# Sign features, v halves and gate taps at the start of an attention, mixing and gating kernel

## The chip, the cores and the metric

The kernel runs on one core of a Trainium2 chip. The core has TensorE (PE, matrix products), VectorE (DVE), ScalarE (ACT), GpSimd (POOL) and SyncE (SP), which here issues the DMA transfers. The metric is the device time of one execution in microseconds. Of the kernel before there are three timed runs: 687.34, 683.41 and 684.14 us, with a median of 684.14.

## The reference

Three layers follow each other, in float32, for a batch of 2.

1. Attention with 8 heads, 768 positions and head size 64. Each q and k row gets a bucket from the signs of its products with six projection vectors, and a score counts only where the buckets of q and k are equal:

```
q_bits = (einsum('bhsd,dk->bhsk', q, proj) > 0);  k_bits likewise
mask   = bucket(q_bits)[:, :, :, None] == bucket(k_bits)[:, :, None, :]
scores = where(mask, q @ k.T / 8, -1e9);  attn = softmax(scores);  x = attn @ v
```

2. A mixing layer on x (768 by 512 for each batch entry): the real part of a Fourier transform over both axes is added to x, then layer norm, a product with w_ch1, relu, a product with w_ch2, and an addition.

3. A gate: a causal convolution over 5 positions with taps conv_w, a sigmoid, times x @ w_val, and a product with w_out.

## The kernel before

Products are exact enough because each float32 operand is split into an upper and a lower fp16 half: the upper half is a rounded copy (`copy_of`, lines 110 to 117), the lower half the rest (`rest_of`, lines 122 to 126). On VectorE the lower half is one instruction; on GpSimd (`"g"`) it is two, a scaling of the input in place and a subtraction. `split` (line 128) does both halves; its string says on which engine each is done ("a" ScalarE, "v" VectorE, "g" GpSimd).

Attention goes over pairs of heads (`g`, four of them in a batch entry), over three units `i` of 256 query rows, over the two heads `hh`, and over two tiles `j` of 128 rows. For each tile, `pair` (line 317) makes scores on TensorE, a row maximum on VectorE (line 338), an exponential on ScalarE (line 343), an upper half on ScalarE and a lower half on GpSimd, and has them transposed, mostly by a DMA that SP issues (line 355). `unit_out` (line 358) multiplies by v and writes x.

Before the first tile of a pair its operands are prepared. `ta` holds the lower parts of q and k and, in 32 rows each, the sign features: they enter the score product, so that unequal buckets get a large penalty. For pairs 1 to 3 this is `prep` (line 230); for pair 0 of batch 0 `prep_first` (line 280) does it head by head. In `prep_first`, for each head: the halves of q and k, their transposes on TensorE, products with the projection (line 307), the sign features by comparison (line 314, one VectorE instruction for head 0, two for head 1), and a copy of 32 rows (line 315) that completes the operand of that head. This copy is kept as a mark, `marks["first", 0]` and `marks["first", 1]`; the exponentials of tiles 0 and 1 are marks too (`marks["first", 2]` and `3`, line 343, on ScalarE). `values` (line 270) makes the halves of v.

The order of the instructions on each engine is worked out ahead of time by a planner, which takes what is ready, earlier lines of the program first. `after_mark` (line 158) names an instruction behind which the ones of its block are to be queued. In the kernel before, the halves of v of pair 0 stand under `marks["first", 0]` (line 273), and so does the splitting in `prep` of pair 1 (line 232); head 1's sign features stand under none, since `MF` is 0 (line 311). The loads of the constants cf, cs and the taps stand under the mark of pair 1's last transposed copy (line 947). `REST` (`'vv'` for batch 0) says on which engine the lower halves of q and k are made, `VH` (`'gg'` for batch 0) the halves of v of pairs 1 to 3. `widen` (line 417) turns the taps from the 64-bit form of the input into float32 with three VectorE instructions; it stands ahead of the loop over the attention of batch 0 (line 962).

The loads of q, k and v of a pair take three buffers, so the load of the next pair's q waits until the last reader of a buffer is done.

Of the kernel before, what the change touches and what calls it, by code (L numbers as in the profile page):

```python
# [15 lines left out]
QS = 2.0 ** 5  # L16
PS = 2.0 ** 3
VS = 2.0 ** 6
# [46 lines left out]
VH = ('gg', 'av')  # L65
PF = 0
MF = 0
PJE = 'g'
REST = ('vv', 'gv')
# [8 lines left out]
def attention_fft_mix_gated_kernel(  # L78
# [31 lines left out]
    def copy_of(o, i, s, eng):  # L110
        if eng == "a":
            return nc.scalar.activation(out=o, in_=i, func=ACTF.Copy, scale=s)  # L112
        if eng == "g":
            return nc.gpsimd.tensor_scalar(o, i, s, 1.0, ALU.mult, ALU.mult)
        if isinstance(s, float) and s == 1.0:
            return nc.vector.tensor_copy(out=o, in_=i)
        return nc.vector.tensor_scalar(o, i, s, None, ALU.mult)  # L117

    def both(o, i0, i1, op, eng):
        return (nc.gpsimd if eng == "g" else nc.vector).tensor_tensor(out=o, in0=i0, in1=i1, op=op)  # L120

    def rest_of(l, h, i, s, eng="v"):
        if eng == "g":
            copy_of(i, i, s, "g")
            return both(l, i, h, ALU.subtract, "g")
        return nc.vector.scalar_tensor_tensor(out=l, in0=i, scalar=s, in1=h, op0=ALU.mult, op1=ALU.subtract)  # L126

    def split(h, l, i, s, how):

        unit = isinstance(s, float) and s == 1.0  # L130
        if len(how) == 3:
            if not unit:
                copy_of(i, i, s, how[0])
            s, unit, how = 1.0, True, how[1:]
        copy_of(h, i, s, how[0])
        if unit:
            return both(l, i, h, ALU.subtract, how[1])
        return rest_of(l, h, i, s, how[1])
# [10 lines left out]
    cw = const.tile([128, KC, K], INT32, name="cw")  # L149
# [5 lines left out]
    moved, last, marks = {}, [], {}  # L155

    @contextmanager
    def after_mark(ins):
        with ExitStack() as stack:
            for i in ins:  # L160
                stack.enter_context(tc.issue_after(i))
            yield


    class Pool:
# [8 lines left out]
        def widen(self, stack, bufs):  # L174
            self.more, self.extra = stack.enter_context(tc.tile_pool(name="q_" + self.name, bufs=bufs, reuse_waits="tile", **self.kw)), bufs
            stack.callback(self.narrow)
# [23 lines left out]
    def attention(b, P, after=None):  # L200
# [15 lines left out]
        def move(o, i, eng):  # L216
            if eng in "vga":
                copy_of(o, i, 1.0, eng)
            else:
                nc.sync.dma_start(out=o, in_=i)  # L220
# [9 lines left out]
        def prep(g):  # L230
            lq, lk, lv = ld.pop(g)
            with after_mark([marks["first", PF]] if not b and g == 1 else []):
                st = [P.a.tile([128, 2 * C, 2, D], FP16, tag="a", name="st", lasting=b and g == 0) for _ in range(2)]
                for y, x in enumerate((lq, lk)):
                    copy_of(st[y][:, :, 1 - y, :], x, QS, "a")
                for y, x in enumerate((lq, lk)):
                    rest_of(st[y][:, :, y, :], st[y][:, :, 1 - y, :], x, QS, REST[b][y])
            if b and g == 2:
                tb = P.spare.tile([128, 2, 2, S], FP16, tag="tb", name="tb")
            else:  # L240
                tb = P.tb.tile([128, 2, 2, S], FP16, tag="tb", name="tb", lasting=b and g == 0)
            ta = P.ta.tile([128, 2, 2, S], FP16, tag="ta", name="ta", lasting=b and g == 0)
            for y in range(2):
                it = st[y].rearrange("p c x d -> p (c x d)")
                if (b, g) in PPE:
                    marks[b, "prep", g] = by_pe(tb[:, y].rearrange("p h t -> p (h t)"), it, PPE[b, g])
                else:
                    marks[b, "prep", g] = nc.sync.dma_start_transpose(
                        out=tb[:, y].rearrange("p h (c t) -> p (h c) t", t=128), in_=it
                    ).ins  # L250
            move(ta[0:64, 0], tb[64:128, 0], QJ[b][0])
            move(ta[0:64, 1], tb[0:64, 1], QJ[b][1])
            for n in range(2):
                r = slice(n * 384, n * 384 + 384)
                bt = P.bt.tile([128, 512], FP32, tag="g", name="bt")[:, 0:384]
                for x in range(3):
                    for hh in range(2):
                        for y in range(2):
                            o = 64 * hh + 32 * y
                            nc.tensor.matmul(  # L260
                                out=bt[o:o + 32, :], lhsT=pj[:, x, y, :], rhs=tb[:, y, hh, r], start=(x == 0), stop=(x == 2)
                            )
                for hh in range(2):
                    o = slice(64 * hh, 64 * hh + 64)
                    nc.vector.tensor_scalar(ta[64:128, 0, hh, r], bt[o, :], lim[o, 0:1], lim[o, 1:2], ALU.is_gt, ALU.mult)
            move(ta[64:96, 1], ta[96:128, 0], QJ[b][2])
            values(g, lv)
            tq[g] = ta, tb

        def values(g, lv):  # L270
            vt = P.vt.tile([128, 2, C, 2, D], FP16, tag="vt", name="vt")
            v2 = vt.rearrange("p h c x d -> p (h c) x d")
            with after_mark([marks["first", PF]] if not b and g == 0 else []):
                split(v2[:, :, 0, :], v2[:, :, 1, :], lv, VS, 'av' if not b and g < 1 else VH[b])
            va[g] = vt

        def first_tiles():
# [2 lines left out]
        def prep_first(hh):  # L280

            ta, tb = tq[0]
            lq, lk, _ = ld[0]
            for y, x in enumerate((lq, lk)):
                if y == 0:
                    p = P.tp.tile([128, 1024], FP16, tag="tp", name="stp")
                else:
                    p = (P.pv if hh else P.bt).tile([128, 1024], FP16, tag="pv" if hh else "g", name="stp")
                x = x[:, hh * C:hh * C + C]
                st = P.a.tile([128, 2 * C, 2, D], FP16, tag="a", name="st")[:, 0:C]  # L290
                copy_of(st[:, :, 1 - y, :], x, QS, "a")
                rest_of(st[:, :, y, :], st[:, :, 1 - y, :], x, QS)
                for c in range(C):
                    nc.tensor.transpose(p[:, c * 128:c * 128 + 128], st[:, c].rearrange("p x d -> p (x d)"), P.idh)
                copy_of(tb[:, y, hh], p[:, 0:S], 1.0, EVF[y][hh])
                copy_of(ta[0:64, y, hh], tb[64 - 64 * y:128 - 64 * y, y, hh], 1.0, SH[2 * hh + y])
            o = slice(64 * hh, 64 * hh + 64)
            if hh:
                bt = [P.tp.tile([128, 512], FP32, tag="tp", name="bt")[:, 0:384] for _ in range(2)]
            else:  # L300
                b2 = P.sc.tile([128, 2, 512], FP32, tag="sc", name="bt")[:, :, 0:384]
                bt = [b2[:, n] for n in range(2)]
            for n in range(2):
                for x in range(3):
                    for y in range(2):
                        i = o.start + 32 * y
                        nc.tensor.matmul(
                            out=bt[n][i:i + 32, :], lhsT=pj[:, x, y, :], rhs=tb[:, y, hh, n * 384:n * 384 + 384],
                            start=(x == 0), stop=(x == 2),
                        )  # L310
            with after_mark([marks["first", MF]] if hh and MF else []):
                t2 = ta[64:128, 0, hh, :].rearrange("p (n r) -> p n r", n=2)
                for w, i in [(t2[:, n], bt[n][o]) for n in range(2)] if hh else [(t2, b2[o])]:
                    nc.vector.tensor_scalar(w, i, lim[o, 0:1], lim[o, 1:2], ALU.is_gt, ALU.mult)
            marks["first", hh] = copy_of(ta[64:96, 1, hh], ta[96:128, 0, hh], 1.0, "v").ins
# [574 lines left out]
    if True:  # L890
# [10 lines left out]
        cwd = tmp.tile([128, KC, K, 2], INT32, name="cwd")  # L901
        cwt = tmp.tile([128, KC, K], INT32, name="cwt")
# [44 lines left out]
        with tc.issue_after(marks[EARLY]):  # L947
# [11 lines left out]
                pre=[work.tile([128, 4 * WP], INT32, tag="t4", name="pre", bufs=4) for _ in range(NPRE)],  # L959
            )  # L960
            next(w)
        widen(cw, cwd[:, :, :, 0], cwd[:, :, :, 1], cwt)
        for i, _ in enumerate(a0):
            if (i % STEP == W0 % STEP and i >= W0) if PACE else i % 4:
                next(w, None)
            if i in (A1LD, A1AT):
                next(a1)
# [136 lines left out]
```

## Time and profile before

| | us |
|---|---|
| median of three timed runs | 684.14 |
| the profiled execution, in all | 682.82 |
| its span, first to last instruction | 681.0 |
| TensorE busy in the span | 578.8 |
| VectorE busy | 521.9 |
| ScalarE busy | 367.0 |
| GpSimd busy | 283.4 |

The profile is of one execution. Busy times are sums over all stages; a table by windows of time shows which engine is full in which stage. A row of a timeline has the start, the duration, the engine, the line of the kernel, the operation, what is written and read, and in brackets how long the engine was idle before and what ended this.

### The profile page before, as it was taken

How to read it: one execution, taken by the hardware profiler on the slowest of the kernel's cores; microseconds unless marked ns; L12 is line 12 of the kernel's file. 1: busy time of each engine (PE TensorE's matmuls, PEld its weight loads, DVE VectorE, ACT ScalarE, POOL GpSimd, SP SyncE). 2: the span in 40 equal slices, each digit the busy share in tenths (PEclk: the TensorE clock that was granted, in tenths of full speed). 3: DMA queues.
4: the chain of work that ended last, by engine and by line, in shares of the span. 5: the costliest groups of instructions: out<-in, count | busy, mean ns of one | idle time of the engine just before them, and what ended most of it. 6: DMA issues, size and time to landing. Idle time of an engine off the chain costs nothing.

```text
span 681.0 us, 13258 instructions
## 1 busy us (share of the span) xinstructions
PE 578.8 (85%) x5078; PEld 443.7 (65%) x5078; DVE 521.9 (77%) x1007; ACT 367.0 (54%) x752; POOL 283.4 (42%) x312
## 2 busy tenths in 40 slices
PE   6787767866537789986999999988999999999997
PEld 3454535544324657665677788877677788888864
DVE  6978797799999898998865369996999256282682
ACT  4997979996764337875888426311334202111242
POOL 3868668875864415767656301260232100000000
PEclk8787779787866689999999999998799999999999
DMA  8989999989776354689785764000000000000001
GB/s 300 236 139 234 210 234 217 225 133 179 149 153 139 110 124 109 148 155 198 139 145 102 135 183 151 6 1 1 1 32 32 32 1 2 2 1 1 1 32 63
DMA packets 177888, 75.84 MB, mean 111 GB/s; under 512 B 162464, under 2 KB 168224, under 8 KB 177824
## 3 DMA queue, kind: packets, MB, share of 16 engines
q1 hardware_dynamic: 177248, 74.88, 50.6%
q8 instruction: 40, 0.66, 0.4%
q14 instruction: 24, 0.20, 0.1%
q10 hardware_dynamic: 576, 0.10, 0.1%
HBM read 32.50 MB, written 3.15 MB: 52 GB/s over the span
## 4 chain that ended last, share of the span: by engine, by line
PE 30%; DVE 13%; ACT 3%; issue 3%; POOL 1%; ACTq 0%; DVEq 0%; POOLq 0%
PE f L729 14%; PE f L712 8%; DVE gt L754 3%; PE op L873 2%; PE vp L848 1%; PE vp L770 1%; ACT a L112 1%; PE op L795 1%; DVE x L126 1%; DVE gt L117 1%; DVE h L694 1%; ACT e L343 1%; DVE cen L644 1%; PE mp L601 1%; DVE gt L821 1%
## 5 line engine op out<-in xcount | busy, mean ns | idle before, releaser
L120 POOL TENSOR_TENSOR a<-e,a 128x384 f16<-128x384 f32 x184 | 174.9, 976 | 93.0 <-ACT a L112 75.7
L712 PE MATMUL f<-un,w 128*128 128x256 f16 x1152 | 135.3, 274 | 3.2 <-DVE h L694 2.7
L729 PE MATMUL f<-h,w 128*128 128x256 f16 x1152 | 133.1, 274 | 0.9 <-DVE h L694 0.9
L712 PEld LDWEIGHTS <-w 128*128 128x128 f16 x1152 | 112.7, 98 | 22.0 <-issue 4.8
L729 PEld LDWEIGHTS <-w 128*128 128x128 f16 x1152 | 112.2, 98 | 17.8 <-issue 3.2
L338 DVE TENSOR_SCALAR_CACHE_REDUCE e<-sc 128x768 f32<-128x768 f32 x96 | 90.5, 949 | 16.1 <-POOL a L120 12.6
L364 PE MATMUL pv<-at,vt 128*64 128x256 f16 x864 | 75.3, 323 | 26.4 <-DMA at<-a 23.4
L343 ACT ACTIVATE e<-e,mx 128x768 f32<-128x768 f32 x96 | 89.1, 929 | 3.7
L364 PEld LDWEIGHTS <-vt 128*64 128x64 f16 x864 | 58.0, 130 | 44.7 <-issue 23.7
L112 ACT ACTIVATE a<-e 128x768 f16<-128x768 f32 x96 | 80.1, 839 | 1.0
L326 PE MATMUL sc<-ta 96*128 96x384 f16 x192 | 51.4, 352 | 29.8 <-DVE e L338 26.0
L694 DVE SCALAR_TENSOR_TENSOR h<-f,h 128x512 f16<-128x512 f32 x48 | 32.7, 686 | 32.7 <-ACT h L693 32.6
L326 PE MATMUL sc<-tb 128*128 128x384 f16 x192 | 51.9, 353 | 0.0
L693 ACT ACTIVATE h<-f 128x512 f16<-128x512 f32 x48 | 28.4, 591 | 43.1 <-PE f L712 42.9
L326 PEld LDWEIGHTS <-ta 96*128 96x128 f16 x192 | 17.0, 100 | 51.1 <-issue 44.6
L700 DVE SCALAR_TENSOR_TENSOR xb<-f,xb 128x256 f32<-128x256 f32 x24 | 13.7, 615 | 43.6 <-PE f L729 43.6
L120 POOL TENSOR_TENSOR w<-wt,w 128x256 f16<-128x256 f32 x40 | 30.1, 764 | 35.4 <-ACT w L112 35.2
L112 ACT ACTIVATE x<-xb 128x256 f16<-128x256 f32 x24 | 11.7, 535 | 54.0 <-DVE xb L700 53.5
L420 DVE SCALAR_TENSOR_TENSOR wt<-ring,wt 128x256 int32<-128x256 int32 (+1 forms) x60 | 37.0, 623 | 0.6
L821 DVE SCALAR_TENSOR_TENSOR gt<-xb,cw,gt 128x256 f32<-128x256 f32 x60 | 37.2, 680 | 0.0
L112 ACT ACTIVATE wt<-wt 128x256 f32<-128x256 f32 x40 | 16.2, 412 | 37.7 <-DVE wt L421 36.7
L421 DVE SCALAR_TENSOR_TENSOR wt<-ring,wt 128x256 int32<-128x256 int32 (+1 forms) x60 | 35.7, 602 | 0.5
(147 smaller groups left out, 930.6 us busy)
## 6 DMA issues: line engine op xcount, KB each, us to landing
ring<-in_moe_w_ch_dram SPq DMA_DIRECT2D x40, 256.0 KB, 3.1
ring<-in_moe_w_ch_dram SPq DMA_DIRECT2D x12, 512.0 KB, 5.0
lv<-in_v_dram SPq DMA_DIRECT2D x8, 384.0 KB, 4.5
out_dram<-ob SPq DMA_DIRECT2D x12, 256.0 KB, 2.0
lq<-in_q_dram SPq DMA_DIRECT2D x7, 384.0 KB, 3.9
lk<-in_k_dram SPq DMA_DIRECT2D x7, 384.0 KB, 4.6
ring<-in_moe_w_val_dram SPq DMA_DIRECT2D x4, 512.0 KB, 5.6
ring<-in_moe_w_out_dram SPq DMA_DIRECT2D x4, 512.0 KB, 3.9
```

The lines of the kernel that those rows point to most:

```text
L112: return nc.scalar.activation(out=o, in_=i, func=ACTF.Copy, scale=s)
L120: return (nc.gpsimd if eng == "g" else nc.vector).tensor_tensor(out=o, in0=i0, in1=i1, op=op)
L326: nc.tensor.matmul(out=s[:, n, 0:384], lhsT=z[0:rows, 0, hh, r], rhs=z[0:rows, 1, hh, n * 384:n * 384 + 384], start=(x == 0), stop=(x == 1),)
L338: nc.vector.tensor_scalar(e.rearrange("p (a b) -> p a b", a=2), s, -(PEN * PEN) / 2, None, ALU.max, ALU.max, accum_out=m[:, 0:1]).ins
L343: marks["first", 2 + j] = nc.scalar.activation(out=e, in_=e, func=ACTF.Exp, bias=m[:, 1:2], scale=SC, accum_out=sums[:, hh, j:j + 1]).ins
L364: nc.tensor.matmul(out=p[64 * hh:64 * hh + 64, :], lhsT=va[g][:, hh, c, x, :], rhs=at[hh][:, :, y, c, :], start=(c == 0 and n == 0), stop= ...
L420: nc.vector.scalar_tensor_tensor(out=tmp, in0=hi, scalar=-0x40000000, in1=tmp, op0=ALU.bitwise_and, op1=ALU.bitwise_or)
L421: return nc.vector.scalar_tensor_tensor(out=dst, in0=lo, scalar=29, in1=tmp, op0=ALU.logical_shift_right, op1=ALU.bitwise_or)
L694: nc.vector.scalar_tensor_tensor(out=h[:, 1, f:f + 2, :], in0=p, scalar=0.0, in1=h[:, 0, f:f + 2, :], op0=ALU.max, op1=ALU.subtract)
L712: nc.tensor.matmul(out=p[:, o, :], lhsT=w1[:, i, kd, (f + o) * 128:(f + o) * 128 + 128], rhs=un[:, j, kd, :], start=(k == 0), stop=(k == 3 ...
L729: nc.tensor.matmul(out=p[:, o, :], lhsT=w2[:, i, f, (d + o) * 128:(d + o) * 128 + 128], rhs=h[:, j, f, :], start=(k == 0), stop=(k == 3 * ...
L821: nc.vector.scalar_tensor_tensor(out=o, in0=src, scalar=cw[:, d, j:j + 1].bitcast(FP32), in1=o, op0=ALU.mult, op1=ALU.add)
```

## The change

Head 1's sign features in `prep_first` now stand under `marks["first", 0]`. v's halves of pair 0 are written out: the upper half on ScalarE under `marks["first", 0]`, the lower half on VectorE under `marks["first", 2]`. v's halves of pair 1 are made on GpSimd and VectorE instead of GpSimd alone. The lower half of pair 1's q is made on GpSimd, that of k stays on VectorE. The widening of the taps is put eight steps into the loop over batch 0's attention.

```
@@ prep
-                    rest_of(st[y][:, :, y, :], st[y][:, :, 1 - y, :], x, QS, REST[b][y])
+                    rest_of(st[y][:, :, y, :], st[y][:, :, 1 - y, :], x, QS, 'gv'[y] if not b and g == 1 else REST[b][y])
@@ values
-            with after_mark([marks["first", PF]] if not b and g == 0 else []):
-                split(v2[:, :, 0, :], v2[:, :, 1, :], lv, VS, 'av' if not b and g < 1 else VH[b])
+            if not b and g == 0:
+                with after_mark([marks["first", 0]]):
+                    copy_of(v2[:, :, 0, :], lv, VS, "a")
+                with after_mark([marks["first", 2]]):
+                    rest_of(v2[:, :, 1, :], v2[:, :, 0, :], lv, VS)
+            else:
+                split(v2[:, :, 0, :], v2[:, :, 1, :], lv, VS, 'gv' if not b and g == 1 else VH[b])
@@ prep_first
-            with after_mark([marks["first", MF]] if hh and MF else []):
+            with after_mark([marks["first", 0]] if hh else []):
@@ the loop over batch 0's attention
-        widen(cw, cwd[:, :, :, 0], cwd[:, :, :, 1], cwt)
         for i, _ in enumerate(a0):
+            if i == 8:
+                widen(cw, cwd[:, :, :, 0], cwd[:, :, :, 1], cwt)
```

## Rows read from the trace of the kernel before

**Rows 1.** The page's first part: busy us, share of the span, instructions.
```profile
PE 578.8 (85%) x5078; PEld 443.7 (65%) x5078; DVE 521.9 (77%) x1007; ACT 367.0 (54%) x752; POOL 283.4 (42%) x312
```

**Rows 2.** Windows, start:end and length; PE, PEld, DVE, ACT, POOL busy; clock, DMA, GB/s.
```profile
14.40:31.80 17.40, 13.31 (x82) 6.53 (x80) 16.11 (x33) 16.90 (x35) 12.54 (x13) 0.70 0.98 264
31.80:57.00 25.20, 20.07 (x180) 14.44 (x182) 18.51 (x37) 24.43 (x54) 17.98 (x21) 0.77 0.93 175
...
520.00:600.00 80.00, 79.63 (x707) 68.93 (x705) 40.86 (x78) 16.09 (x30) 3.33 (x3) 1.00 0.02 8
```

**Rows 3.** VectorE's timeline, 9.8 to 16.5 us.
```profile
9.80 0.74 DVE L116 COPY ta<-tb 64x768 f16<-64x768 f16 x2 [0.45 <-ACT tb L112]
...
10.84 1.07 DVE L314 TENSOR_SCALAR ta<-bt,lim 64x768 f16<-64x768 f32 x1 [0.29 <-PE bt L307]
...
11.94 1.29 DVE L314 TENSOR_SCALAR ta<-bt,lim 64x384 f16<-64x384 f32 x2
...
13.26 0.35 DVE L116 COPY ta<-ta 32x768 f16<-32x768 f16 x1
13.64 0.96 DVE L126 SCALAR_TENSOR_TENSOR vt<-lv,vt 128x768 f16<-128x768 f32 x1
14.52 0.17 DVE L419 TENSOR_SCALAR cwt<-cwd 128x20 int32<-128x20 int32 x1
...
15.53 0.96 DVE L338 TENSOR_SCALAR_CACHE_REDUCE e<-sc 128x768 f32<-128x768 f32 x1
...
16.41 0.95 DVE L126 SCALAR_TENSOR_TENSOR st<-lq,st 128x768 f16<-128x768 f32 x1
```

**Rows 4.** TensorE's timeline: the first scores, and the transposes of pair 1's q.
```profile
13.66 0.48 PE L326 MATMUL sc<-ta 96*128 96x384 f16 x2 [2.12 <-DVE ta L116]
13.99 0.49 PE L326 MATMUL sc<-tb 128*128 128x384 f16 x2
...
17.78 1.49 PE L226 MATMUL atp<-idh,st 128*128 128x128 f16 x12
```

**Rows 5.** ScalarE's timeline: v, pair 1's q and k, a marked copy, an upper half.
```profile
8.23 0.84 ACT L112 ACTIVATE vt<-lv 128x768 f16<-128x768 f32 x1 [0.73 <-DMA lv<-in_v_dram]
8.98 0.79 ACT L112 ACTIVATE tb<-stp 128x768 f16<-128x768 f16 x1
14.41 0.84 ACT L112 ACTIVATE st<-lq 128x768 f16<-128x768 f32 x1 [4.63 <-DMA lq<-in_q_dram]
15.45 0.84 ACT L112 ACTIVATE st<-lk 128x768 f16<-128x768 f32 x1 [0.20 <-DMA lk<-in_k_dram]
...
23.50 0.81 ACT L112 ACTIVATE tb<-atp 128x768 f16<-128x768 f16 x1
...
27.43 0.85 ACT L112 ACTIVATE a<-e 128x768 f16<-128x768 f32 x1
```

**Rows 6.** SP's timeline: the issues of cf and of the next v.
```profile
3.51 0.47 SPq L948 DMA_DIRECT2D cf<-in_dft_f_dram  x1
...
14.66 0.38 SPq L213 DMA_DIRECT2D lv<-in_v_dram  x1
```

**Rows 7.** GpSimd's timeline: first lower half, pair 1's v, and q in batch 1.
```profile
18.75 2.01 POOL L120 TENSOR_TENSOR a<-e,a 128x384 f16<-128x384 f32 x2 [9.83 <-ACT mx L342]
...
23.75 0.83 POOL L114 TENSOR_SCALAR lv<-lv 128x768 f32<-128x768 f32 x1
24.66 1.65 POOL L120 TENSOR_TENSOR vt<-lv,vt 128x768 f16<-128x768 f32 x1
...
125.74 2.23 POOL L120 TENSOR_TENSOR st<-lq,st 128x768 f16<-128x768 f32 x1
```

**Rows 8.** VectorE's timeline: k's lower half in batch 1, beside GpSimd's q.
```profile
124.98 1.49 DVE L126 SCALAR_TENSOR_TENSOR st<-lk,st 128x768 f16<-128x768 f32 x1 [0.77 <-ACT st L112]
```

**Rows 9.** Two idle times further on, VectorE's and ScalarE's.
```profile
40.06 0.62 DVE L380 TENSOR_TENSOR xb<-pv,xb 128x256 f32<-128x256 f32 x1 [3.92 <-ACT xb L112]
...
59.16 0.60 ACT L112 ACTIVATE w<-wt 128x512 f16<-128x512 f32 x1 [2.12 <-DVE wt L421]
```

## The prediction

> **What bounds the kernel now.** I read the page's busy line first: TensorE 85%, VectorE 77%, ScalarE 54%, GpSimd 42% over 681.0 us [rows 1]. An average over unlike stages says little, so I went on to the table by windows [rows 2]. The reader is to see that the full engine changes: from 14.4 to 57 us it is ScalarE, 16.90 of 17.40 us and then 24.43 of 25.20; near the end, from 520 to 600, it is TensorE, 79.63 of 80. The change touches none of the late work. All it edits lies in the first 30 us, so what it can do is move the beginning of attention in batch 0, and what is gained there has to pass through ScalarE's full queue.
>
> The timelines of the engines at the start show the path. VectorE does the sign features of head 0 (10.84, 1.07 us), then both halves of head 1's (11.94 to 13.23), and only then the 32-row copy that completes head 0's operand (13.26) [rows 3]. The first score matmul waits for this copy until 13.66, an idle of 2.12 us on TensorE [rows 4]. Behind the copy VectorE does v's lower half (13.64, 0.96 us), the first piece of the taps (0.17), head 1's copy and the other taps, and only at 15.53 the first row maximum, though its four score matmuls ended at 14.48 (13.99 + 0.49) [rows 3, 4].
>
> **Sign features of head 1.** The mark is a VectorE instruction and so are the two held instructions, so it takes hold. They leave the way of head 0's copy: 13.23 - 11.94 = 1.3 us.
>
> **v's lower half.** The diff puts it under a mark that is a ScalarE instruction (the exponential of the first tile), while the lower half runs on VectorE. Does such a mark hold? The kernel before has the same pattern twice. The loads of cf, cs and the taps stand under the mark of the second pair's last transposed copy, which ScalarE ran at 23.50; SP issued cf at 3.51 [rows 5, 6]. And v's upper half on ScalarE stood under the VectorE mark of 13.26 and ran at 8.23 [rows 3, 5]. So a mark orders its own engine alone. The edit therefore doesn't move v's lower half back; it takes away the hold that it had, and it can go as soon as v's upper half is done (8.23 + 0.84 = 9.07). It costs 0.96 us wherever it lands. In VectorE's hole at 9.36 to 9.80, ahead of the copies at 9.80, it pushes these by 0.5 us, of which 0.29 is absorbed by the idle before 10.84: head 0's copy is 0.2 later. Behind 10.84 it costs the copy the whole 0.96. Bounds of both edits together: 1.3 - 0.96 = 0.3 to 1.3 - 0.2 = 1.1 us. I take 1.1, the first place, since ScalarE runs v's upper half before the copy (8.98) that the VectorE copies at 9.80 wait for, so the lower half is ready before they are [rows 3, 5]. Its end also frees the buffer for the next v: SP issued that load at 14.66, right behind it [rows 6]; it now goes earlier, behind the loads of q and k in the same queue.
>
> **First maximum.** With head 0's copy at 12.2 to 12.5 and four score matmuls of 0.82 us together, the scores end at 13.4. VectorE still has 1.3 us of head 1's signs: the maximum starts near 13.9, not 15.53, 1.6 us earlier.
>
> **Taps.** Three instructions of about 0.17 us leave the stretch from 14.52 [rows 3]: some 0.5 us. Nothing reads them before the gating, after the whole of attention and mixing; where they go they cost at most those 0.5.
>
> **Swap of q and v in pair 1.** v's upper half stays on POOL. POOL loses the scaling and the subtraction of the lower half (0.83 + 1.65 us at 23.75 and 24.66) and takes the same two for q: nothing in sum, but q's come while POOL is idle, since its first lower half starts at 18.75 after 9.83 us of idle [rows 7]. q's upper half ends at 15.25 [rows 5], so they run 15.25 to 17.7. VectorE loses 0.95 us at 16.41 and takes 0.96 later, plus what the two engines cost each other: a lower half of this shape takes 0.95 alone (16.41) and k's 1.49 beside the same POOL pair in batch 1 (124.98), and POOL's subtraction 2.23 instead of 1.65 [rows 3, 7, 8]. That is +0.54 on VectorE and +0.58 on POOL. VectorE in sum: -0.95 + 0.96 + 0.54 - 0.5 = 0.05; bounds -1.5 (no mutual cost, v's in the hole at 36) to +1.4 (k's lower half held from 16.29 to the end of POOL's subtraction, 17.7).
> The Trainium skill, page "SBUF — State Buffer", section "Who interferes with whom", says that a VectorE instruction with two SBUF inputs and a GpSimd one that reads SBUF exclude each other: the later one blocks for the whole of the first. The rows of batch 1 agree: 124.98 starts inside POOL's copy, and POOL's subtraction is longer by about as much as what was left of it. By that rule k's lower half would pay 1.4 here and not 0.54.
>
> q's lower half is ready at 17.7 instead of 17.36. TensorE's transposes of it stood at 17.78 [rows 4], so this is hidden; if POOL took 0.58 more, they wait 0.5 us. The load of the next q goes the same 0.4 us later.
>
> **What of it reaches the end.** ScalarE takes the first maximum, but it has to make the upper halves of pair 1's q and k as well, which wait for DMA until 14.41 and 15.45 [rows 5]. From 14.40 to 31.80 it is idle for 0.50 us, from 31.80 to 57 for 0.77 [rows 2]. An earlier maximum fills these 0.50 (0.20 of it stands before 15.45, most of the rest before the first maximum's use); it can't make ScalarE's own work shorter. The other 0.77 belongs to later waits. Nor does POOL's relief reach further: v's pieces (to 24.66 + 1.65 = 26.3) hold up the third tile's lower half, but the first unit needs the fourth tile as well, whose upper half ScalarE ends at 27.43 + 0.85 = 28.3 whatever POOL does [rows 5, 7]. So of 1.6 us I keep **0.5**, with bounds 0 and 1.3 (0.50 + 0.77), if the queues stay as they are. On the profiled execution, 681.0 span and 682.82 in all, this is 682.3. That execution lies 1.3 below the median of 684.14, which the result is compared with: 684.14 - 0.5 = **683.6**, own range 682 to 685.5. It is no change that a measurement could tell: that needs about 0.5%, 3.4 us.
>
> **Rivals.**
> *A hole further on closes (faster).* The queues are ordered ahead of time, and moving three VectorE instructions and four POOL ones reorders what follows. VectorE stands 3.92 us at 40.06 for the first unit's output while its next maxima could run, and ScalarE 2.12 at 59.16 for weights that VectorE had not yet widened [rows 9]. If the first unit's output no longer blocks the maxima, that is 3.9 + 0.5: 684.14 - 4.4 = 679.7; with the second hole 677.6. For it: v's two POOL pieces stand just ahead of the third tile's lower half. Against: the fourth tile, above, and a hole that closes can open again elsewhere. Chance 0.30.
> *The marks hold after all.* v's lower half then waits for the first exponential (16 to 17), the next v's load goes from 14.66 to some 17.3, and pair 1's v that much later; the maximum still gains. 683.9. Chance 0.07.
> *The two engines exclude each other.* k's lower half and pair 1's v each pay 1.4: 684.14 + 2.9 - 0.5 = 686.5. For it, the rows of batch 1; against, k's high half may be planned behind. Chance 0.06. This is what the page named above would make of it.
> *TensorE waits for POOL's q (slower).* In TensorE's queue q's twelve transposes (17.78) stand ahead of later scores [rows 4]. If POOL's queue has the first tile's lower half (18.75, 2.01 us) [rows 7] before q's two pieces, these end at 20.76 + 2.48 = 23.2 and the scores stand still for 23.2 - 17.78 = 5.4 us: 684.14 + 5.4 - 0.5 = 689.0. It decides from the point where q's subtraction ends after 18.7. Against: q lands at 14.41, 3 us before the first high half. Chance 0.12.
>
> **How the numbers follow.** The forecast holds 0.45, the rivals 0.30, 0.07, 0.06 and 0.12. Faster is the first rival, 0.30. Slower is the last, 0.12, and 0.03 for the upper part of the exclusion. The rest, 0.55, is no change. The range goes down to 677.6 (both holes) and up to 688.0, short of the last rival's 689.0.
>
> **What would show it.** Head 0's last copy at 12.2 to 12.9, the first score matmul right behind it, the first maximum by 14.2. v's lower half before 13 us, not after the first exponential. q's POOL pieces before the first tile's lower half, and k's lower half longer than 0.95. ScalarE full from 14.4 to 31.8 with less than 0.3 us idle. The prediction is wrong if ScalarE's exponentials at 30 to 60 us are more than 1.3 us earlier, if the wait of VectorE for the first unit's output is gone, or if TensorE waits for the transposes of q.

## The result and the profile after

The changed kernel takes 689.85 us (median of 7 runs, 688.65 to 691.79), the kernel before 683.41 (7 runs, 682.68 to 687.34) beside it. The ratio is 1.0081, with a 95% interval of 1.0061 to 1.0102: slower by 0.8%, about 5.5 us (the ratio, here and below, is not quite that of the medians, which differ by 6.4 us here). The forecast was 683.6 us and no change; its range ended at 688.0. The profiled execution has a span of 689.9 us, before 681.0.

The page's busy line answers to [rows 1]: the work is the same (the counts are equal), but VectorE is busy for 6.6 us more and GpSimd for 2.6, TensorE for 3.1 less.

```profile
PE 575.7 (83%) x5078; PEld 439.8 (64%) x5078; DVE 528.5 (77%) x1007; ACT 367.6 (53%) x752; POOL 286.0 (41%) x312
```

VectorE's timeline of the first 27 us, and the first unit's output, answers to [rows 3, 9].

```profile
9.12 0.94 DVE L126 SCALAR_TENSOR_TENSOR vt<-lv,vt 128x768 f16<-128x768 f32 x1
...
12.22 0.18 DVE L424 TENSOR_SCALAR cwt<-cwd 128x20 int32<-128x20 int32 x1 [0.29 <-DMA cwd<-in_conv_t_dram]
12.43 0.35 DVE L116 COPY ta<-ta 32x768 f16<-32x768 f16 x1
12.82 1.29 DVE L319 TENSOR_SCALAR ta<-bt,lim 64x384 f16<-64x384 f32 x2
14.14 0.18 DVE L425 SCALAR_TENSOR_TENSOR cwt<-cwd,cwt 128x20 int32<-128x20 int32 x1
14.35 0.35 DVE L116 COPY ta<-ta 32x768 f16<-32x768 f16 x1
14.74 0.18 DVE L426 SCALAR_TENSOR_TENSOR cw<-cwd,cwt 128x20 int32<-128x20 int32 x1
14.95 0.96 DVE L343 TENSOR_SCALAR_CACHE_REDUCE e<-sc 128x768 f32<-128x768 f32 x1
...
16.71 2.38 DVE L126 SCALAR_TENSOR_TENSOR st<-lk,st 128x768 f16<-128x768 f32 x1
...
25.44 1.24 DVE L126 SCALAR_TENSOR_TENSOR vt<-lv,vt 128x768 f16<-128x768 f32 x1
...
41.30 0.62 DVE L385 TENSOR_TENSOR xb<-pv,xb 128x256 f32<-128x256 f32 x1 [4.36 <-ACT xb L112]
```

GpSimd's timeline answers to [rows 7]. q's two pieces come ahead of the first tile's lower half, as forecast.

```profile
15.72 0.84 POOL L114 TENSOR_SCALAR lq<-lq 128x768 f32<-128x768 f32 x1 [6.90 <-ACT st L112]
16.64 1.65 POOL L120 TENSOR_TENSOR st<-lq,st 128x768 f16<-128x768 f32 x1
18.79 1.96 POOL L120 TENSOR_TENSOR a<-e,a 128x384 f16<-128x384 f32 x2 [0.50 <-ACT a L112]
```

TensorE's timeline answers to [rows 4]. The fourth tile's scores now stand ahead of q's transposes (in the kernel before, behind them), and neither waits for GpSimd.

```profile
17.19 0.85 PE L331 MATMUL sc<-ta 96*128 96x384 f16 x2
...
18.47 1.19 PE L226 MATMUL atp<-idh,st 128*128 128x128 f16 x12
```

ScalarE's timeline answers to [rows 5]: the upper halves of pair 1's q and k still wait for their loads, and the first exponential stands behind them.

```profile
14.80 0.84 ACT L112 ACTIVATE st<-lq 128x768 f16<-128x768 f32 x1 [5.86 <-DMA lq<-in_q_dram]
15.84 0.84 ACT L112 ACTIVATE st<-lk 128x768 f16<-128x768 f32 x1 [0.20 <-DMA lk<-in_k_dram]
...
16.81 0.93 ACT L348 ACTIVATE e<-e,mx 128x768 f32<-128x768 f32 x1
```

It starts no earlier than in the kernel before:

```profile
16.76 0.94 ACT L343 ACTIVATE e<-e,mx 128x768 f32<-128x768 f32 x1
```

The windows of the attention's start answer to [rows 2] (start:end and length; PE, PEld, DVE, ACT, POOL busy; clock, DMA, GB/s). ScalarE has 1.01 us idle in the first, where it had 0.50, and 2.65 in the second, where it had 0.77.

```profile
14.40:31.80 17.40, 11.10 (x77) 5.75 (x76) 15.63 (x27) 16.39 (x34) 13.36 (x14) 0.83 0.94 247
31.80:57.00 25.20, 16.85 (x152) 10.87 (x149) 20.16 (x40) 22.55 (x50) 16.01 (x19) 0.77 0.86 170
```

So the front part came out much as forecast: v's lower half at 9.12, head 0's copy at 12.43, q on GpSimd early. Only 1.24 us of the loss (41.30 against 40.06) stand at the first unit's output. The rest has to be looked for later. Three views of one line each show the stages: the additions of batch 0's mixing (first and last start), those of batch 1's, and the start of batch 1's first products with w_ch2, its mixing layer's second weight matrix (in a window from 536 to 554 us). Before:

```profile
L609 DVE TENSOR_TENSOR xb<-mp,xb x12: 591/606/625, 212.1 to 239.8; 128x256 f32<-128x256 f32 x12
...
L609 DVE TENSOR_TENSOR xb<-mp,xb x12: 590/610/631, 447.0 to 471.1; 128x256 f32<-128x256 f32 x12
...
L729 PE MATMUL f<-h,w x132: 272/273/273, 539.6 to 553.9; 128*128 128x256 f16 x132
```

After:

```profile
L614 DVE TENSOR_TENSOR xb<-mp,xb x12: 597/614/639, 220.7 to 239.9; 128x256 f32<-128x256 f32 x12
...
L614 DVE TENSOR_TENSOR xb<-mp,xb x12: 591/615/630, 452.3 to 478.1; 128x256 f32<-128x256 f32 x12
...
L734 PE MATMUL f<-h,w x55: 272/273/273, 548.1 to 554.0; 128*128 128x256 f16 x55
```

Batch 0's mixing ends at the same time. Batch 1's ends 7.0 us later, and its products with w_ch2 start 8.5 later; the span is 8.9 longer. So at these products nearly all of the loss is there, and most of it shows hundreds of microseconds behind the edits.

### The profile page after: what moved, and what is told of

The parts are those of the page before. It is cut to its first block, busy times and chain, and to the rows that moved or that the text cites. A ratio compares the mean times of both kernels' runs of the same rounds, so it can differ in the third digit from the quotient of the medians.

```text
span 689.9 us, 13261 instructions
## 1 busy us (share of the span) xinstructions
PE 575.7 (83%) x5078; PEld 439.8 (64%) x5078; DVE 528.5 (77%) x1007; ACT 367.6 (53%) x752; POOL 286.0 (41%) x312
## 4 chain that ended last, share of the span: by engine, by line
PE 38%; DVE 25%; issue 3%; DMA 3%; ACT 2%; POOL 1%; SPq 0%; ACTq 0%; DVEq 0%; POOLq 0%
PE f L734 14%; PE f L717 12%; DVE wt L425 2%; DVE gt L759 2%; PE op L878 2%; PE pv L369 2%; DVE e L343 2%; DVE z L120 2%; PE sc L331 2%; DVE wt L426 2%; DVE cen L649 1%; PE vp L853 1%; DVE wt L424 1%; PE vp L775 1%; DVE h L699 1%
## 5 line engine op out<-in xcount | busy, mean ns | idle before, releaser
L717 PE MATMUL f<-un,w 128*128 128x256 f16 x1152 | 137.5, 276 | 2.6 <-DVE h L699 2.0
L369 PE MATMUL pv<-at,vt 128*64 128x256 f16 x864 | 70.3, 310 | 29.2 <-DMA at<-a 26.1
L369 PEld LDWEIGHTS <-vt 128*64 128x64 f16 x864 | 55.6, 125 | 47.2 <-issue 24.4
L120 POOL TENSOR_TENSOR w<-wt,w 128x256 f16<-128x256 f32 x40 | 31.9, 803 | 40.2 <-ACT w L112 40.2
L331 PEld LDWEIGHTS <-ta 96*128 96x128 f16 x192 | 17.9, 101 | 43.5 <-issue 36.7
L425 DVE SCALAR_TENSOR_TENSOR wt<-ring,wt 128x256 int32<-128x256 int32 (+1 forms) x60 | 40.3, 678 | 0.5
L426 DVE SCALAR_TENSOR_TENSOR wt<-ring,wt 128x256 int32<-128x256 int32 (+1 forms) x60 | 37.0, 622 | 0.5
```

The costliest lines, as they stand in the source:

```text
L331: nc.tensor.matmul(out=s[:, n, 0:384], lhsT=z[0:rows, 0, hh, r], rhs=z[0:rows, 1, hh, n * 384:n * 384 + 384], start=(x == 0), stop=(x == 1),)
L369: nc.tensor.matmul(out=p[64 * hh:64 * hh + 64, :], lhsT=va[g][:, hh, c, x, :], rhs=at[hh][:, :, y, c, :], start=(c == 0 and n == 0), stop= ...
L425: nc.vector.scalar_tensor_tensor(out=tmp, in0=hi, scalar=-0x40000000, in1=tmp, op0=ALU.bitwise_and, op1=ALU.bitwise_or)
L426: return nc.vector.scalar_tensor_tensor(out=dst, in0=lo, scalar=29, in1=tmp, op0=ALU.logical_shift_right, op1=ALU.bitwise_or)
L717: nc.tensor.matmul(out=p[:, o, :], lhsT=w1[:, i, kd, (f + o) * 128:(f + o) * 128 + 128], rhs=un[:, j, kd, :], start=(k == 0), stop=(k == 3 ...
```

## The experiments

The theories at the start. A: the time is lost because the planner, given other instructions at the start, orders everything behind them anew. B: GpSimd's q holds VectorE's k. C: the hold on v that the edit takes away was worth something. D: a moved step does harm where it now stands.

First, a reading of the two programs: with v's two new marks left out (and its old one), every engine gets the changed kernel's order, instruction by instruction. The marks on another engine do nothing, as the prediction held.

**One edit alone, ordered by the planner.** Four kernels, each before with one edit:

```
s_sign    with after_mark([marks["first", 0]] if hh else []):         # head 1's sign features
s_vfree   v's halves of pair 0 under no mark
s_q       rest_of(..., 'gv'[y] if not b and g == 1 else REST[b][y])   # q's lower half, pair 1
s_v1      split(..., 'gv' if not b and g == 1 else VH[b])             # v's lower half, pair 1
```

> The kernel before with the hold on head 1's sign features alone. Theory A (the loss comes with the new order of the queues, not with the work of an edit): an irregular change between -5 and +7 us, though the first maximum comes 1 us earlier. Theory B (the loss is GpSimd's q, which blocks VectorE's k): no loss, -1 to +0.5 us, since q and v of pair 1 are untouched. Theory C (the loss is the lost hold of v's lower half): no loss either, -1 to +0.5 us.

> The kernel before with the hold on v's halves of pair 0 taken away, nothing else. Theory A: irregular, between -5 and +7 us. Theory B: -1 to +0.5 us. Theory C: most of the loss, +4 to +7 us.

> The kernel before with pair 1's q lower half on GpSimd, nothing else. Theory A: irregular, between -5 and +7 us. Theory B: most of the loss, +4 to +7 us, with k's lower half at about 2.4 us instead of 0.95. Theory C: -1 to +1 us.

> The kernel before with the lower half of pair 1's v on VectorE, nothing else. Theory A: irregular, between -5 and +7 us. Theories B and C: a gain of up to 1 us or nothing, since 2.5 us leave GpSimd's full stretch.

| | median us | ratio to before, 95% |
|---|---|---|
| s_sign | 689.46 | 1.0086 [1.0051, 1.0121] |
| s_vfree | 695.33 | 1.0164 [1.0129, 1.0198] |
| s_q | 688.64 | 1.0077 [1.0054, 1.0099] |
| s_v1 | 699.99 | 1.0233 [1.0195, 1.0271] |

Each of these edits alone costs about as much as the whole change, or more. Their sum is 5.6%, the whole, which moves the taps as well, costs 0.8%; prices of steps would add. s_vfree (11 us) and s_v1 (16 us) even lie above the range that was expected by theory A, which ended at +7. s_sign and s_vfree run exactly before's instructions, so there an order alone is paid for. That speaks for A, but a local harm (C, D) is not excluded yet.

**The same edits in the order of before.** A helper fixes each engine's order by chaining its instructions; only the instructions under test are moved in the list.

```
for x, y in zip(q, q[1:]):        # q: one engine's instructions in the wanted order
    tc.add_manual_dep(y, x.name, NoSync)
...
VectorE in before  signs h0, signs h1, copy h0, v, tap, copy h1, tap, tap, max 1, q, max 2, k, max 3
o_sign             signs h0, copy h0, signs h1, v, tap, copy h1, tap, tap, max 1, q, max 2, k, max 3
o_early            v (at 9 us), signs h0, copy h0, signs h1, copy h1, max 1, q, max 2, k, taps, max 3
o_all              as o_early; q on GpSimd; v of pair 1 on VectorE behind the sixth maximum
o_qv               as before; q on GpSimd; v of pair 1 as in o_all
```

> Every engine's queue held in the order that the kernel before has, but for one step: head 0's operand copy goes ahead of head 1's two sign features, as in the single edit that cost 0.86%. Theory A (the loss is the new order further down the queues): no loss, -1.5 to +0.7 us against the kernel before. Theory D (the moved step itself does the harm, by what it sets off on the chip): the same loss as the single edit, +4 to +7 us.

> As o_sign, and v's lower half of pair 0 goes where the changed kernel has it (ahead of the copies at 9.8 us), and the taps go behind pair 1's k. Theory A: -2 to +0.5 us. Theory D: +4 to +12 us, as the single edits cost 0.86% and 1.64%.

> All of the changed kernel's work, with the steps of o_early, q's lower half of pair 1 on GpSimd ahead of its first tile, v's lower half of pair 1 on VectorE behind the sixth maximum, and all other queues in the order of the kernel before. Theory A: -2 to +1.5 us (the upper end is k's lower half held for 1.4 us by GpSimd). Theory D: +4 to +8 us, like the change.

> The swap of q and v of pair 1 alone, in the order of the kernel before. Theory A: -1 to +1.5 us. Theory B (the loss is GpSimd's q beside VectorE's k): +4 to +7 us. Theory D: +4 to +17 us, as the single edits of q and v cost 0.77% and 2.33%.

o_sign: 683.92 us, 0.9998 [0.9977, 1.0019]. o_early: 683.75, 0.9993 [0.9976, 1.0010]. o_all: 688.15, 1.0056 [1.0036, 1.0077]. o_qv: 687.59, 1.0042 [1.0022, 1.0062].

Beside s_sign and s_vfree this settles C, and D for three steps: the sign step, the freed v and the taps cost nothing where they stand, and gain nothing that shows. The local gain is there, and it shrinks at once: in o_early the first maximum is at 14.00 against 15.53 [rows 3], the first unit's output at 39.71 against 40.06 [rows 9], and batch 0's last mixing addition starts at 239.9 against 239.8. VectorE of o_early:

```profile
14.00 0.96 DVE L337 TENSOR_SCALAR_CACHE_REDUCE e<-sc 128x768 f32<-128x768 f32 x1
...
39.71 0.61 DVE L379 TENSOR_TENSOR xb<-pv,xb 128x256 f32<-128x256 f32 x1 [3.92 <-ACT xb L112]
```

The swap, however, costs 0.4 to 0.6% even in the old order: 2.9 us (o_qv) and 3.8 (o_all), above the ranges of theory A, which ended at +1.5, and a little below those of B and D. VectorE's timeline of o_all shows the places (k's lower half, the taps, the third maximum, pair 1's v):

```profile
16.31 2.38 DVE L126 SCALAR_TENSOR_TENSOR st<-lk,st 128x768 f16<-128x768 f32 x1 [0.45 <-ACT st L112]
18.61 0.88 DVE L418 TENSOR_SCALAR cwt<-cwd 128x20 int32<-128x20 int32 x1
19.53 0.84 DVE L419 SCALAR_TENSOR_TENSOR cwt<-cwd,cwt 128x20 int32<-128x20 int32 x1
20.40 0.80 DVE L420 SCALAR_TENSOR_TENSOR cw<-cwd,cwt 128x20 int32<-128x20 int32 x1
21.12 0.94 DVE L337 TENSOR_SCALAR_CACHE_REDUCE e<-sc 128x768 f32<-128x768 f32 x1
...
26.66 1.42 DVE L126 SCALAR_TENSOR_TENSOR vt<-lv,vt 128x768 f16<-128x768 f32 x1
```

In o_qv, where k comes later, the instructions that stand beside q's pieces pay instead, a copy of 0.35 us and a tap of 0.18:

```profile
15.05 0.87 DVE L116 COPY ta<-ta 32x768 f16<-32x768 f16 x1
15.96 1.52 DVE L419 SCALAR_TENSOR_TENSOR cwt<-cwd,cwt 128x20 int32<-128x20 int32 x1
...
19.48 0.95 DVE L126 SCALAR_TENSOR_TENSOR st<-lk,st 128x768 f16<-128x768 f32 x1
```

**The swap in parts, and the order alone.** o_allt is o_all with the taps before head 1's copy, beside an idle GpSimd; o_qt is the same without v of pair 1; o_v1 is o_early with v of pair 1 alone. l_qv is o_early's work in the planner's own order.

```
o_allt, o_qt   ..., signs h1, taps, copy h1, max 1, max 2, k, max 3, ...
l_qv           sign features held, v's mark removed, taps at step 8 of the loop; no order given
```

> As o_all (all of the change's work, each queue in the order of before), but the three taps instructions stand before head 1's 32-row copy, where GpSimd is idle, and not behind pair 1's k. Theory 1, the swap's price is paid at the places where VectorE meets GpSimd: in o_all the taps took 0.88, 0.84 and 0.80 us beside GpSimd's first lower halves instead of 0.17 each, so they return to 0.17 and the third maximum to about 19.1 instead of 21.1; k's lower half still takes 2.4. 688.15 - 2.0 = 686.2 us. Theory 2, the price lies in what the swap does to the other queues (GpSimd's later work, TensorE's wait for q): the time stays at 688.

> Order of before, with the sign features behind head 0's copy, v's lower half freed, the taps before head 1's copy, and of the swap only q's lower half of pair 1 on GpSimd; pair 1's v stays on GpSimd whole. Theory 1: k's lower half takes 2.4 instead of 0.95, q's 0.96 leaves VectorE, the taps stand 0.5 ahead of the first maximum: 683.75 + 1.45 - 0.96 + 0.5 = 684.7 us. Theory 2, q on GpSimd holds up TensorE's transposes and with them the scores: 686.5 or more.

> As o_early (sign features, v's lower half and taps moved, order of before) with only pair 1's v changed: its lower half on VectorE behind the sixth maximum, its upper half on GpSimd. Theory 1: the lower half meets GpSimd's first-tile work there, as in o_all where it took 1.42, and delays the next maxima by that: 683.75 + 1.4 = 685.2 us. Theory 2, GpSimd's relief of 0.83 + 1.65 us lets the next lower halves come sooner: 682.5 to 683.7.

> The same work as o_early (sign features held, v's lower half freed, taps eight steps into the loop, no swap), in the planner's own new order. Theory A, the order behind the first 30 us costs: 688 to 695 us, against 683.75 for o_early with the same instructions. Rival: the single edits alone were unlucky draws that cancel when they come together: 683 to 685.

o_allt: 686.72 us, 1.0034 [1.0016, 1.0052]. o_qt: 686.33, 1.0019 [1.0004, 1.0035]. o_v1: 685.78, 1.0023 [1.0006, 1.0041]. l_qv: 689.46, 1.0076 [1.0052, 1.0099].

Over o_early (0.9993) q's half costs 0.26% or 1.8 us and v's half 0.30% or 2.1 us; both together 0.41% or 2.8 us, and the taps in a bad place bring that to 0.63% in o_all, though the intervals of o_all and o_allt overlap. These differences are hardly larger than their noise, and in q's half there is also the place of the taps, which in o_qt put the first maximum at 14.66 and in o_early stand behind k. The traces support them: the first unit's output stands at 39.71 in o_early, at 41.12 in o_qt and at 41.83 in o_v1. VectorE of o_qt:

```profile
41.12 0.62 DVE L379 TENSOR_TENSOR xb<-pv,xb 128x256 f32<-128x256 f32 x1 [3.93 <-ACT xb L112]
```

v's half is a little above theory 1's 1.4 us: it meets GpSimd's lower halves of the exponentials, takes 1.63 us instead of 0.95, and one of them in turn seems held (2.50 us for two, 1.78 for the two before). VectorE in o_v1:

```profile
25.58 1.63 DVE L126 SCALAR_TENSOR_TENSOR vt<-lv,vt 128x768 f16<-128x768 f32 x1
```

GpSimd in o_v1:

```profile
25.48 2.50 POOL L120 TENSOR_TENSOR a<-e,a 128x384 f16<-128x384 f32 x2 [1.44 <-ACT a L112]
```

And l_qv beside o_early is theory A with equal instructions: 0.8% for an order.

**Where q's half is paid in the old order.** In o_qt k's lower half takes 2.21 us, but TensorE stands as well: q's transposes wait for GpSimd, and the fourth tile's scores are queued behind them. TensorE of o_qt:

```profile
17.99 1.46 PE L226 MATMUL atp<-idh,st 128*128 128x128 f16 x12 [0.87 <-POOL st L120]
19.25 0.84 PE L325 MATMUL sc<-ta 96*128 96x384 f16 x2
```

VectorE of o_qt:

```profile
16.54 2.21 DVE L126 SCALAR_TENSOR_TENSOR st<-lk,st 128x768 f16<-128x768 f32 x1
...
20.77 0.96 DVE L337 TENSOR_SCALAR_CACHE_REDUCE e<-sc 128x768 f32<-128x768 f32 x1 [1.14 <-PE sc L325]
```

In o_qlate k stands behind the third maximum, where GpSimd has ended its subtraction.

```
o_qt           max 1, max 2, k, max 3, max 4
o_qlate        max 1, max 2, max 3, k, max 4
```

> As o_qt (order of before; q's lower half of pair 1 on GpSimd), but k's lower half stands one place later in VectorE's queue, behind the third maximum, so that it meets only the end of GpSimd's subtraction. It should take about 1.2 us instead of 2.2, and the third maximum should start at 16.9 to 17.1 instead of 18.67. Theory V, VectorE's block is the price: 686.3 - 1.3 = 685.0 us. Theory P, TensorE's queue is the price (the fourth tile's scores stand behind the transposes of q, which wait for GpSimd until 17.9): the fourth maximum stays at 20.8 and the time at 686.3.

VectorE of o_qlate:

```profile
17.09 0.96 DVE L337 TENSOR_SCALAR_CACHE_REDUCE e<-sc 128x768 f32<-128x768 f32 x1 [0.65 <-PE sc L325]
18.09 0.96 DVE L126 SCALAR_TENSOR_TENSOR st<-lk,st 128x768 f16<-128x768 f32 x1
20.75 0.96 DVE L337 TENSOR_SCALAR_CACHE_REDUCE e<-sc 128x768 f32<-128x768 f32 x1 [1.71 <-PE sc L325]
```

k takes 0.96 again and the third maximum comes 1.6 us earlier (17.09 against 18.67), but the fourth stays where it was, waiting for its scores, as theory P has it. The time, 685.24 us, 1.0015 [0.9997, 1.0034], can't be told from o_qt's 1.0019, but theory V's gain of 1.3 us, 0.2%, would lie inside these intervals too. So up to the fourth maximum VectorE's block is real but not what ends last; TensorE's queue is. In o_early, with q's lower half on VectorE, these transposes ran earlier, as its TensorE timeline shows:

```profile
16.32 1.46 PE L226 MATMUL atp<-idh,st 128*128 128x128 f16 x12
17.58 0.85 PE L325 MATMUL sc<-ta 96*128 96x384 f16 x2
```

The fourth maximum is at 19.32 in o_early, at 20.77 in o_qt, and at 20.58 in before. Against o_early these 1.45 us agree with the 1.41 at the first unit's output. Against before they don't: there o_qt is 0.2 late at the fourth maximum and 1.06 at that output. So this wait is not shown to be all of q's price.

**Where the order loses.** Two orders of the same instructions are joined: up to batch 0's last mixing addition, with all that it needs, by one order, behind it by the other.

```
x_afirst  changed kernel's order first, o_allt's behind     x_lfirst  l_qv's first, o_early's behind
x_alast   o_allt's first, changed kernel's behind           x_llast   o_early's first, l_qv's behind
x_v7      s_vfree's order to the eighth unit output, o_early's behind
```

> The changed kernel's work. Each queue in the changed kernel's order up to batch 0's last mixing output (and all that this needs), behind it in the order of before. Theory L, the new order loses behind batch 0: its trace has that output at 239.9 us as before had (239.8), against 244.4 for o_allt, so the time is at o_allt's 686.7 or up to 4.5 below: 682.2 to 686.7 us. Theory F, it loses in the first part: 689 to 690.

> The other way round: o_allt's order up to batch 0's last mixing output, behind it the changed kernel's order. Theory L: the loss comes, 689 to 692 us. Theory F: 686 to 687.

> No swap (the work of o_early): the planner's order of l_qv up to batch 0's last mixing output, behind it the order of before. Theory L: l_qv had that output at 236.1 us, o_early at 239.9; if the rest takes as long as in before, 683.8 - 3.8 = 680.0 us, faster than before. Middle: the gain is given back at a later wait, 682 to 684. Theory F: 687 or more.

> No swap: o_early's order up to batch 0's last mixing output, behind it the planner's order of l_qv. Theory L: 688 to 693 us. Theory F: 683 to 684.5.

> The work of o_early. The planner's order of s_vfree up to the eighth unit output (which it had at 114.8 us against 117.0 for o_early), behind it the order of before. If the later stages keep the lead: 683.8 - 2.2 = 681.6 us, faster than both kernels. If the lead was bought by work pushed behind the joint, as in x_lfirst: 684 to 690.

| | median us | ratio to before, 95% |
|---|---|---|
| x_afirst | 685.75 | 1.0029 [1.0011, 1.0046] |
| x_alast | 693.38 | 1.0142 [1.0120, 1.0163] |
| x_lfirst | 690.87 | 1.0108 [1.0089, 1.0126] |
| x_llast | 688.35 | 1.0073 [1.0053, 1.0094] |
| x_v7 | 684.11 | 1.0006 [0.9989, 1.0024] |

For the changed kernel theory L holds: with its own order up to 240 us and the old one behind, it costs 1.0029 and not 1.0081; its order behind 240 us brings the rest. What is left has the size of the swap in the old order (o_allt's 1.0034), but not its path: in x_afirst the first unit's output is only 0.4 us late (40.49) and q's transposes wait for nothing. x_alast agrees in its direction, but at 693.38 us it missed its range (689 to 692): the parts do not add up to the whole, so a joined order may have a price of its own too. The same lines of x_afirst as above, for batch 1:

```profile
L608 DVE TENSOR_TENSOR xb<-mp,xb x12: 591/615/632, 450.7 to 475.3; 128x256 f32<-128x256 f32 x12
...
L728 PE MATMUL f<-h,w x104: 272/273/273, 542.7 to 554.0; 128*128 128x256 f16 x104
```

The products with w_ch2 start at 542.7 and not at 548.1; these 5.4 us are nearly the whole difference of the spans (684.2 and 689.9). They grow step by step: the changed kernel is 1.6 us behind x_afirst at the first of batch 1's mixing additions (452.3 against 450.7), 2.8 at the last, and 5.4 at these products, behind batch 0's gating. Which move in the queues starts it was not tried and stays open.

For l_qv theory L fails: either half of its order loses alone. x_lfirst is the instructive miss. Batch 0's mixing did end early, at 236.2, and the time was still 7.4 us up. Its rows of batch 1's unit outputs (first and last), of batch 0's mixing and of the products with w_ch2:

```profile
L379 DVE TENSOR_TENSOR xb<-pv,xb x12: 416/607/624, 187.4 to 406.1; 128x256 f32<-128x256 f32 x12
...
L608 DVE TENSOR_TENSOR xb<-mp,xb x12: 603/616/629, 217.1 to 236.2; 128x256 f32<-128x256 f32 x12
...
L728 PE MATMUL f<-h,w x64: 272/273/273, 547.0 to 553.9; 128*128 128x256 f16 x64
```

The unit outputs in before:

```profile
L380 DVE TENSOR_TENSOR xb<-pv,xb x12: 417/610/633, 178.0 to 399.3; 128x256 f32<-128x256 f32 x12
```

And in x_afirst:

```profile
L379 DVE TENSOR_TENSOR xb<-pv,xb x12: 418/609/635, 190.3 to 402.8; 128x256 f32<-128x256 f32 x12
```

While batch 0's mixing was early, batch 1's attention had been put back: by 9.4 us at its first output and still 6.8 at its last (406.1 against 399.3), and the products with w_ch2 are 7.4 late. A late first output alone is not the price, though: x_afirst's is 12.3 late, but its last one only 3.5 and its products 3.1. That the early mixing was bought by the late attention fits these rows; no run moved the one without the other. x_v7 takes over s_vfree's lead at the eighth unit output (2.2 us in s_vfree's trace), and nothing of it reaches the end. No version beats the kernel before by more than its interval.

## Why the prediction was wrong

*Head 1's sign features, v's lower half.* Right. The same-engine mark held, the cross-engine ones did not; v went into the hole at 9.12, and head 0's copy to 12.43 (forecast 12.2 to 12.5). That this copy fell into its range is in part luck: a tap that was not foreseen there stands ahead of it and waited for its load until 12.22; in o_early, without it, the copy is at 11.91.

*Taps.* Wrong as a step. The edit puts them later in the program, not in VectorE's queue: two stand at 14.14 and 14.74, ahead of the first maximum, and so does head 1's copy (14.35), which the sum for the maximum left out. So this is at 14.95 and not at 13.9. Its 14.00 in o_early was worth nothing that shows either.

*Swap.* Its term is mis-sized. VectorE's sum was taken as 0.05, with 0.54 for the mutual cost; k paid 2.38 - 0.95 = 1.43 us and pair 1's v 0.29 (in o_v1 0.68). (With 1.41 in place of 0.54 that sum gives 0.9, not the 1.4 that stands as its bound.) The Trainium skill's rule on the shared ports ("SBUF — State Buffer", "Who interferes with whom"), weighed there, gave 1.4 for k: the trace agrees, with 1.43 (GpSimd's subtraction went on for 1.58 us behind k's start). The same section of the Trainium skill says that copies can contend too, and o_qv's copy, 0.87 us for 0.35, agrees. In the old order k alone does not pay. "This is hidden" was reckoned against the 17.78 of before; with the maxima earlier, as in o_early, those transposes could come at 16.3, and GpSimd's 17.9 was then the late one (o_qt, 0.87 us of waiting). In the changed kernel itself this wait is absent; what the swap costs there, and by which path, stays open. In the old order the swap costs 2 to 4 us (o_allt, o_all), not 0; the rival that named the exclusion, 686.5 us, had this size (o_allt 686.7) and was given 0.06. The equal sum is in part luck: pair 1's v did not pay 1.4.

*What of it reaches the end.* This is the step that failed: "So of 1.6 us I keep 0.5 ... if the queues stay as they are." The 0.5 was about right at the first unit's output (0.35 in o_early) and gone by batch 0's mixing. But the queues did not stay as they were, and over half of the loss is that: 0.81 - 0.29 = 0.52%, 3.6 us, belongs to the order behind 240 us, as x_afirst splits it. The prediction saw that the queues would be reordered, but held it only as a chance of gain (the first rival, 0.30). It gave a new order no price of its own, and the trace of before could not show one, having only one order. Six other orders that the planner gave (the changed kernel's, l_qv and the four single edits; three of them hold the swap or a half of it, which costs 0.3 to 0.6% in the old order) cost 0.76 to 2.33%, none gained: among these before's order is a favourable one.

*ScalarE full with less than 0.3 us idle* did not come: 1.01 us are idle. The first exponential stayed behind the upper halves of pair 1's q and k, which wait for their loads, and started at 16.81, in the kernel before at 16.76, so the earlier maximum found nothing to fill.

*The rival that TensorE waits for GpSimd's q* did not come in the changed kernel, where the planner put the fourth tile's scores ahead of the transposes. In the old order it came, but with 0.87 us of waiting in o_qt (1.45 in o_all, 2.31 in o_allt) and not 5.4, since GpSimd's queue had q first. Its 689.0 us, near the 689.85 measured, is luck.

## What to carry to other kernels

Where a planner orders the queues, a small edit is two changes: its own work, and a new order for all that follows. Try it in the old order first; only there is its own price seen by itself. Don't trust a lead at one milestone until the work that was put back for it has been looked up. And when several steps of an edit gain together, reckon each step's cover against the new times of its neighbours, not against the old.

## What was not expected of the hardware

Beside GpSimd's scalings and subtractions VectorE's smallest instructions were held as well: int32 ones of 20 elements a row took 0.80 to 1.52 us beside them instead of 0.17 to 0.18, and a 32-row copy 0.87 instead of 0.35. They ended about when GpSimd's instruction did: o_qv's tap began at 15.96, and GpSimd's subtraction ran from 15.80 to 17.44. Here, then, a short instruction cost what was left of the long one, however little it does itself. Not every one pays: the changed kernel's third maximum (19.02), which reads its scores from PSUM, took 0.94 us beside GpSimd's lower halves.
